# Heads made ready a pair ahead and weight rounding split into two stages in a fused clustered-attention and feed-forward kernel

## The chip, the cores and the metric

The kernel runs on one core of a Trainium2 chip. The metric is device microseconds (us) of one execution, the median of the runs. In this text PE is the matrix engine (TensorE), DVE the vector engine, ACT the scalar engine, POOL the general-purpose engine (GpSimd), and SP the engine that only issues DMAs. Each engine works through its own queue in order and waits for the others by semaphores.

## The reference

Attention in which a query sees only keys of its own cluster, followed by a feed-forward layer whose activation is h - tanh(h):

```python
# q, k, v: (4, 8, 768, 64) f32; centroids: (8, 16, 64) f32
q_assign = argmax(q_n @ c_n.T)          # nearest of 16 centroids of the head, by cosine
k_assign = argmax(k_n @ c_n.T)
mask = q_assign[:, :, :, None] == k_assign[:, :, None, :]
scores = where(mask, (q @ k.T) / 8, -1e9)
attn = softmax(scores)
x = (attn @ v).transpose(0, 2, 1, 3).reshape(3072, 512)
h = x @ w_in                            # w_in (512, 2048), float64 in memory
out = (h - tanh(h)) @ w_out             # w_out (2048, 512), float64 in memory
```

## The kernel before

Two heads make a pair (128 partitions: 2 heads of 64 dimensions); there are 4 batches of 4 pairs, pairs n = 0 to 15. Queries are taken in two halves of 384. The main loop runs over 96 **steps** `(n, half, s)`: for each batch, each half, each of its 4 pairs, and each of 3 thirds of the keys (s = 0, 1, 2; two key tiles of 128 each). Twelve steps, all of one batch and half, are called a **block** here, blocks 0 to 7. Step k runs on the engines in this order:

- `begin(following)`: the scores of step k+1. PE multiplies two key tiles with the queries into PSUM tiles `sc` (pool `ps_s`, two buffers), ACT takes the exponential in place (L317).
- `value`: PE multiplies the weights `e` of step k with the values (L348). After the last third, `total` adds up the denominators on PE (`den`, L361), ACT copies both results, POOL tests each denominator against two bounds (L371 and L372, twice each), and DVE later divides (`divide`, three reciprocals L378 and a product L381).
- `select` of step k+1: DVE multiplies the exponentials with the test "query's cluster code equals key's cluster code" (L326, four instructions, into `e`, two buffers), POOL adds the rows of `e` up (L335, L339).
- Beside these, the feed-forward layer of the block before (`ffn_items`, 28 items spread over the 12 steps: 16 `up` items with `h` on PE L393, tanh on ACT L398 and `g = h - tanh` on DVE L400, then 12 `project` items with `o` on PE L406). Block 0 has no such work; the items of block 7 run after the last step, as a tail.

Work to be done by DVE and so on in step k (`todo`) is handed out between the feed-forward items of that step through `between`: an item's matmuls come first, then its share of `todo`, then the `g` of an `up` item.

**Preparing a pair** (`prepare`, stages 0 to 3): `turn` transposes q and k on PE into two `ps_s` tiles (L233) and copies q with ACT (L239), k with DVE (L241); `similar` multiplies with the centroids (L251) and ACT copies (L256); `route` transposes on PE (L263) and takes the arg-max in four DVE instructions (L271 to L278); `publish` transposes the codes of the queries on PE (L287), DVE copies them, and SP writes them to memory (`q_codes`); `spread` reads them back into all partitions (`row`). Stages 0 to 2 run in the thirds s = 0, 1, 1 and stages 3 and `spread` at the start of s = 2 of the step group just before the pair is first used. So pairs 1, 2, 3 of a batch are prepared in its first half (even block), pair 0 of the next batch at the end of the second half (odd block).

**The weights** lie in memory as float64 and are rounded to f32 by hand in 32 pieces (`round_weights`): ACT scales the low words (L146), DVE builds the bits in two instructions (L147, L151), POOL adds (L154), DVE masks small numbers in two more (L155, L159). One piece per step in block 0, three per step in block 1. Pieces are fetched by POOL's DMA queue into two `raw` buffers. Projections, `h`, have two PSUM banks (`ps_f`).

The first lines issue the loads: q and k of pair 0, v of pair 0, q and k of pair 1, the other v, and last the centroids; then the centroid norms on DVE, then pair 0 is prepared.

## Time and profile before

| | |
|---|---|
| runs | median 1259.69 us, 1257.97 to 1261.23 |
| profiled execution | 1258.72 us, span of its instructions 1256.9 us |
| PE busy | 1084.5 us (86% of the span) |
| DVE busy | 530.5 us (42%) |
| POOL busy | 486.7 us (39%) |
| ACT busy | 294.4 us (23%) |
| chain of work that ended last | PE 76%, DVE 14%, POOL 5%, the rest 1% or less each |

The profile is read by stretches, because the stages have different limits: the start, up to the first `select` (at 39.74 us); block 0, which has no feed-forward work; block 1, in which two thirds of the weights are rounded; blocks 2 to 7; and the tail. For each stretch one asks how busy PE is, and where it is not, what ended its waits. Spans of POOL are rough. The rows for this stand in the section after the next.

### The profile page before, as it was taken

To read this page: it belongs to the slowest core of one execution; us is meant where nothing else is said; L and a number is where in the kernel's file an instruction comes from. 1 tells how busy PE (TensorE), PEld (TensorE's weight loads), DVE (VectorE), ACT (ScalarE), POOL (GpSimd) and SP (SyncE) were. 2 spreads that over 40 slices of the span, in tenths; PEclk is the share of its full clock that TensorE was granted. 3 is DMA by queue.
4 is the path that set the end of the run, shared out by engine and by line. 5 is a ranking of instruction groups with operands and counts; after the bars stand their busy time and mean duration, and the time that the engine had idled before them with its cause. 6 is when DMAs were issued, how large, how long until landed. Compare 5 with 4: busy or idle time off the path is not lost.

```text
span 1256.9 us, 10657 instructions
## 1 busy us (share of the span) xinstructions
PE 1084.5 (86%) x3842; PEld 503.2 (40%) x3842; DVE 530.5 (42%) x902; ACT 294.4 (23%) x475; POOL 486.7 (39%) x358
## 2 busy tenths in 40 slices
PE   1554587688989899999988999999898899999997
PEld 1222133333444434544344434544444344544553
DVE  1666676676334433443335332443343433442210
ACT  1222232222123212222222222322222212321110
POOL 0455475565323343353333433454232343444000
PEclk9777778888999999999999999999999999999999
DMA  6232214231211101111111110012110001000000
GB/s 158 58 86 68 77 65 125 84 109 55 59 34 38 38 34 29 26 26 41 48 38 26 38 42 21 26 26 55 42 31 12 10 33 34 13 9 9 9 8 20
DMA packets 88525, 55.44 MB, mean 44 GB/s; under 512 B 77008, under 2 KB 77200, under 8 KB 88464
## 3 DMA queue, kind: packets, MB, share of 16 engines
q1 hardware_dynamic: 83856, 37.89, 11.4%
q0 software_dynamic: 4608, 16.78, 4.3%
q8 instruction: 33, 0.54, 0.2%
q14 instruction: 28, 0.23, 0.1%
HBM read 48.27 MB, written 6.39 MB: 43 GB/s over the span
## 4 chain that ended last, share of the span: by engine, by line
PE 76%; DVE 14%; POOL 5%; ACT 1%; issue 1%; DMA 1%; SPq 1%; POOLq 0%; DVEq 0%; ACTq 0%
PE o L406 26%; PE h L393 24%; PE sc L312 11%; PE av L348 10%; POOL rest L154 3%; DVE w_in L151 2%; DVE e L326 2%; PE pt L233 2%; PE den L361 2%; SPq L223 1%; DVE den L378 1%; POOL is_in L371 1%; PE sim L251 1%; DVE w_in L147 1%; DVE w_out L151 1%
## 5 line engine op out<-in xcount | busy, mean ns | idle before, releaser
L393 PE MATMUL h<-xT,w_in 128*128 128x384 f32 x1024 | 354.7, 501 | 26.3 <-DVE g L400 26.3
L339 POOL TENSOR_TENSOR sum<-sum,e 128x768 f32<-128x768 f32 x128 | 232.1, 1813 | 348.9 <-DVE e L326 346.4
L406 PE MATMUL o<-w_out,g 128*128 128x512 f32 x768 | 343.7, 599 | 0.0
L326 DVE SCALAR_TENSOR_TENSOR e<-row,code,sc 128x384 f32<-128x384 f32 x384 | 213.2, 608 | 229.6 <-ACT sc L317 99.8
L393 PEld LDWEIGHTS h<-xT,w_in 128*128 128x128 f32 x1024 | 193.6, 194 | 183.3 <-issue 34.6
L406 PEld LDWEIGHTS o<-w_out,g 128*128 128x128 f32 x768 | 141.6, 190 | 187.1 <-issue 186.0
L317 ACT ACTIVATE sc<-sc 128x768 f32<-128x768 f32 x192 | 145.9, 793 | 271.2 <-PE sc L312 270.6
L312 PE MATMUL sc<-t,t 64*128 64x384 f32 x768 | 173.4, 571 | 37.0 <-DVE e L326 23.3
L400 DVE TENSOR_TENSOR g<-h,th 128x384 f32<-128x384 f32 x128 | 71.1, 556 | 224.0 <-ACT th L398 223.8
L371 POOL TENSOR_SCALAR is_in<-den 128x384 f32<-128x384 f32 x64 | 75.0, 1171 | 222.0 <-ACT den L368 219.0
L348 PE MATMUL av<-e,vals 128*64 128x384 f32 x768 | 158.3, 537 | 0.0
L398 ACT ACTIVATE th<-h 128x384 f32<-128x384 f32 x128 | 62.7, 490 | 321.1 <-PE h L393 321.1
L312 PEld LDWEIGHTS sc<-t,t 64*128 64x128 f32 x768 | 73.3, 206 | 123.2 <-issue 74.7
L378 DVE RECIPROCAL den<-den 128x128 f32<-128x128 f32 x96 | 83.3, 917 | 57.1 <-POOL is_in L371 57.1
L348 PEld LDWEIGHTS av<-e,vals 128*64 128x64 f32 x768 | 50.2, 147 | 101.8 <-issue 98.0
L335 POOL TENSOR_TENSOR sum<-e 128x768 f32<-128x768 f32 x32 | 57.8, 1806 | 40.2 <-DVE e L326 40.2
L372 POOL TENSOR_TENSOR ok<-ok,is_in 128x384 f32<-128x384 f32 x64 | 63.8, 997 | 5.3
L413 ACT COPY osb<-o 128x512 f32<-128x512 f32 x24 | 14.0, 585 | 168.8 <-PE o L406 168.8
L233 PE MATMUL pt<-ident,x 128*128 128x128 f32 x192 | 30.0, 304 | 26.1 <-issue 16.3
L287 PE MATMUL sim<-ident,code 128*12 128x128 f32 x16 | 5.1, 320 | 48.7 <-DVE code L278 48.7
L233 PEld LDWEIGHTS pt<-ident,x 128*128 128x128 f32 x192 | 24.9, 156 | 35.6 <-issue 22.4
L241 DVE COPY t<-pt 128x768 f32<-128x768 f32 x16 | 15.3, 956 | 40.8 <-PE pt L233 40.8
(60 smaller groups left out, 368.6 us busy)
## 6 DMA issues: line engine op xcount, KB each, us to landing
row<-q_codes SPq DMA_DIRECT2D x32, 384.0 KB
raw<-in_moe_w_in_dram POOLq DMA_DIRECT2D x16, 512.0 KB, 4.2
raw<-in_moe_w_out_dram POOLq DMA_DIRECT2D x16, 512.0 KB, 3.8
x<-in_q_dram SPq DMA_DIRECT2D x32, 192.0 KB
x<-in_k_dram SPq DMA_DIRECT2D x32, 192.0 KB
vals<-in_v_dram SPq DMA_DIRECT2D x32, 192.0 KB
out_dram<-osb SPq DMA_DIRECT2D x24, 256.0 KB
q_codes<-qc SPq DMA_DIRECT2D x16, 6.0 KB
```

What stands on the lines that cost most here:

```text
L233: nc.tensor.transpose(out=pt[:, j // HCH, (j % HCH) * P : (j % HCH + 1) * P], in_=x[:, j].rearrange("p h d -> p (h d)"), identity=ident,)
L312: nc.tensor.matmul(sc[:, h, 0:TB], lhsT=turned[n, 1][r].rearrange("p a n -> p (a n)")[:, j * P : (j + 1) * P], rhs=turned[n, 0][r, half], ...
L317: nc.scalar.activation(out=sc[:, :, 0:TB], in_=sc[:, :, 0:TB], func=ACT.Exp, scale=SCALE)
L326: nc.vector.scalar_tensor_tensor(out=e[:, h], in0=rows[n, half][:, h], scalar=codes[n][:, 1, j // HCH, h, j % HCH : j % HCH + 1], in1=sc[: ...
L339: nc.gpsimd.tensor_tensor(out=s, in0=s, in1=pair[:, i], op=ALU.add)
L348: nc.tensor.matmul(avs[n, half][h * D : h * D + D], lhsT=vals[n][:, j, h], rhs=e[:, i, h], start=(j == 0), stop=(j == NCH - 1),)
L371: nc.gpsimd.tensor_scalar(out=is_in, in0=t, scalar1=bound, scalar2=None, op0=op)
L372: nc.gpsimd.tensor_tensor(out=ok, in0=ok, in1=is_in, op=ALU.mult)
L378: nc.vector.reciprocal(out=t[:, c], in_=t[:, c])
L393: nc.tensor.matmul(h, lhsT=w_in[i][:, c, o * P : (o + 1) * P], rhs=xT[b, half][:, c], start=(c == 0), stop=(c == CD - 1),)
L400: nc.vector.tensor_tensor(out=gs[i][:, o], in0=h, in1=th, op=ALU.subtract)
L406: nc.tensor.matmul(acc[sub], lhsT=gs[i][:, o, sub * P : (sub + 1) * P], rhs=w_out[i][:, o], start=(i == 0 and o == 0), stop=(i == NQ4 - 1 ...
```

## The change

- **Pairs a pair ahead.** The stages of a pair are put on a list (`ready`) that assigns them to steps: pairs 0 and 1 before the loop, pairs 2 and 3 in block 0, pairs 4, 5, 6 in block 1; from then on pair 3 of a batch in the first three steps of its even block, and pairs 0, 1, 2 of the next batch in the odd block. The stages go to the end of the step's `todo`, `turn` copies both q and k with ACT, and `spread` is issued two steps before use. The codes travel as bf16.
- **Start.** Centroids are loaded first, on ACT's queue; three weight pieces are fetched at once; q and k of pair 1 come before v of pair 0; the transposes of pair 0 stand ahead of the centroid norms; two pieces are rounded before the loop. v is loaded with the heads apart, so that each partition gets 1536 bytes in a row.
- **Weight rounding in two stages.** `round_weights` ends with POOL's addition, and the last two DVE instructions (`guard_weights`) run one call later; three `raw` buffers; `rest` shares the output's buffers.
- **Range check by sums.** In place of four POOL instructions per pair and half, POOL adds the denominators up (`wholes`) and their reciprocals (`inverses`); the bounds are tested once at the end.
- **PSUM.** `ps_f` gets three banks and also holds `den`; `ps_a` keeps one.
- **Output stores** move from SP's queue to POOL's.

The core of the diff:

```diff
-        rawp = cx.enter_context(tc.tile_pool(name="rawp", bufs=2))
+        rawp = cx.enter_context(tc.tile_pool(name="rawp", bufs=3))
-        ps_a = cx.enter_context(tc.tile_pool(name="ps_a", bufs=2, space=PSUM))
-        ps_f = cx.enter_context(tc.tile_pool(name="ps_f", bufs=2, space=PSUM))
+        ps_a = cx.enter_context(tc.tile_pool(name="ps_a", bufs=1, space=PSUM))
+        ps_f = cx.enter_context(tc.tile_pool(name="ps_f", bufs=3, space=PSUM))
...
             nc.gpsimd.tensor_tensor(out=rest, in0=bits, in1=rest, op=ALU.add)
+
+        def guard_weights(n: int):
...
+            hi = raws.pop(n).rearrange("p (n two) -> p n two", two=2)[:, :, 1]
             nc.vector.tensor_scalar(
                 out=bits, in0=hi, scalar1=20, scalar2=0x7FF,
                 op0=ALU.logical_shift_right, op1=ALU.bitwise_and,
             )
             nc.vector.scalar_tensor_tensor(
-                out=dst, in0=bits, scalar=float(F32_LEAST), in1=rest.bitcast(F32),
+                out=dst, in0=bits, scalar=float(F32_LEAST), in1=rests.pop(n).bitcast(F32),
...
-            is_in = okp.tile([P, TB], F32, name="is_in")
-            for bound, op in ((SUM_LEAST, ALU.is_ge), (SUM_MOST, ALU.is_le)):
-                nc.gpsimd.tensor_scalar(out=is_in, in0=t, scalar1=bound, scalar2=None, op0=op)
-                nc.gpsimd.tensor_tensor(out=ok, in0=ok, in1=is_in, op=ALU.mult)
+            nc.gpsimd.tensor_tensor(out=wholes, in0=wholes, in1=t, op=ALU.add)
...
+                nc.gpsimd.tensor_tensor(out=inverses, in0=inverses, in1=dens.pop((n, half)), op=ALU.add)
...
+        def before(n: int):
+
+            yield lambda: (turn(n, 0, nc.scalar), turn(n, 1, nc.scalar), load(n + 2))
+            yield lambda: similar(n)
+            yield lambda: route(n)
+            yield lambda: publish(n)
...
+            if b == 0:
+                at = (p - 2) * NS + 1
+            elif p < HP - 1:
+                at = ((2 * b - 1) * HP + p + 1) * NS
+            else:
+                at = 2 * b * HP * NS
+            for i, stage in enumerate(before(n)):
+                ready.setdefault(at + i - (i > 1), []).append((i, stage))
...
+            if guarded < rounded - 1 or guarded == len(PIECES) - 1:
+                guard_weights(guarded)
+                guarded += 1
+                fetch()
...
+        centroid_load()
+        load(0)
+        for i in range(3):
+            fetch()
+        constants()
+        load(1)
...
+        turn(0, 0, nc.scalar)
+        turn(0, 1, nc.vector)
+        centroid_norms()
+        similar(0)
+        turn(1, 0, nc.scalar)
+        load(2)
+        route(0)
+        publish(0)
+        spread(0, 0)
+        weights_on()
         begin(steps[0])
+        turn(1, 1, nc.scalar)
+        load(3)
+        similar(1)
+        weights_on()
         for i in range(2):
             select(*steps[0][:2], i)
+        route(1)
+        publish(1)
...
+            if 3 in stages:
+                stages.pop(3)()
+            if after and after[2] == 0:
+                spread(*after[:2])
...
+            todo += [stages[i] for i in sorted(stages)]
```

What this makes of the order of instructions, at two places. First DVE in block 1, where three pieces of the weights are rounded in a step (`w_in_70`, `w_out_71` and the like are pieces of the two weight matrices, `raw` the fetched words, `rest` POOL's sum, `g` the activation). Before:

```order
L147 TENSOR_SCALAR w_in_70<-raw 128x512
L151 SCALAR_TENSOR_TENSOR w_in_70<-raw,w_in_70 128x512
L155 TENSOR_SCALAR w_in_70<-raw 128x512
L159 SCALAR_TENSOR_TENSOR w_in_70<-w_in_70,rest 128x512
L400 TENSOR_TENSOR g<-h,th 128x384
L147 TENSOR_SCALAR w_out_71<-raw 128x512
L151 SCALAR_TENSOR_TENSOR w_out_71<-raw,w_out_71 128x512
L155 TENSOR_SCALAR w_out_71<-raw 128x512
L159 SCALAR_TENSOR_TENSOR w_out_71<-w_out_71,rest 128x512
```

Now, where the last piece of `w_in` and the first of `w_out` meet:

```order
L146 TENSOR_SCALAR w_out_72<-raw 128x512
L150 SCALAR_TENSOR_TENSOR w_out_72<-raw,w_out_72 128x512
L162 TENSOR_SCALAR w_in_71<-raw 128x512
L166 SCALAR_TENSOR_TENSOR w_in_71<-w_in_71,rest 128x512
L409 TENSOR_TENSOR g<-h,th 128x384
```

The two last instructions of a piece now stand behind the two first of the next piece.

Second PE in block 2, at the preparation of a pair (`pt` are the transposes of `turn`, `sim<-t` the product of `similar`, `sim<-ident,simt` the transposes of `route`, `sim<-ident,code` that of `publish`, `sc` and `av` scores and values, `h` the feed-forward layer). Before:

```order
L393 MATMUL h<-xT,w_in_67 128x384 x8
L233 MATMUL pt<-ident,x_624 128x128 x6
L233 MATMUL pt<-ident,x_627 128x128 x6
L393 MATMUL h<-xT,w_in_67 128x384 x4
L312 MATMUL sc<-t_1430,t_1439 128x384 x4
...
L251 MATMUL sim<-t_1594,bd 32x384 x2
L251 MATMUL sim<-t_1603,bd 32x384 x2
L393 MATMUL h<-xT,w_in_68 128x384 x4
L263 MATMUL sim<-ident,simt 128x128 x3
L287 MATMUL sim<-ident,code 12x128
L312 MATMUL sc<-t_1594,t_1603 128x384 x4
```

Now:

```order
L402 MATMUL h<-xT,w_in_68 128x384 x12
L244 MATMUL pt<-ident,x_1366 128x128 x6
L244 MATMUL pt<-ident,x_1369 128x128 x6
L323 MATMUL sc<-t_1139,t_1148 128x384 x4
...
L402 MATMUL h<-xT,w_in_69 128x384 x8
L262 MATMUL sim<-t_1672,bd 32x384 x2
L262 MATMUL sim<-t_1681,bd 32x384 x2
L274 MATMUL sim<-ident,simt 128x128 x3
L298 MATMUL sim<-ident,code 12x128
L323 MATMUL sc<-t_1355,t_1364 128x384 x4
```

The feed-forward matmuls that stood between the stages now stand ahead of them; `publish` follows `route` directly, as before, with nothing of another item between.

## Rows read from the trace of the kernel before

**Rows 1.** Busy time by stretch: length, PE, PEld, DVE, ACT, POOL; clock, DMA, GB/s.
```profile
39.74:182.31 142.57, 81.43 (x310) 33.44 (x311) 92.72 (x134) 35.82 (x53) 77.40 (x61) 0.74 0.25 72
182.31:286.22 103.91, 74.58 (x235) 35.06 (x234) 72.66 (x121) 28.21 (x50) 59.82 (x55) 0.89 0.35 106
286.22:349.86 63.64, 59.87 (x209) 25.11 (x209) 29.47 (x47) 14.64 (x23) 29.24 (x20) 0.95 0.19 52
349.86:1167.29 817.43, 776.71 (x2835) 362.65 (x2834) 318.08 (x542) 199.94 (x323) 318.24 (x215) 0.99 0.11 30
1049.11:1167.29 118.18, 118.18 (x409) 55.21 (x410) 44.72 (x76) 27.87 (x46) 51.55 (x35) 1.00 0.04 13
1167.29:1256.90 89.61, 82.59 (x226) 42.30 (x224) 10.00 (x19) 10.19 (x20) 0.00 (x0) 0.98 0.04 13
...
349.86:496.31 146.45, 135.13 (x507) 63.21 (x505) 57.49 (x98) 35.57 (x57) 53.34 (x36) 0.98 0.13 34
```

**Rows 2.** Timeline of the start: start, length, engine, line, operation [idle before, releaser].
```profile
20.88 0.23 DVE L178 TENSOR_TENSOR sq<-cen 128x64 f32<-128x64 f32 x1 [19.33 <-DMA cen<-in_centroids_dram]
...
25.15 2.77 PE L233 MATMUL pt<-ident,x 128*128 128x128 f32 x12
...
39.74 2.19 DVE L326 SCALAR_TENSOR_TENSOR e<-row,code,sc 128x384 f32<-128x384 f32 x4 [4.96 <-DMA row<-q_codes]
```

**Rows 3.** DMA queue of the loads, 2 to 9 us: packets, MB, share.
```profile
q1 hardware_dynamic: 3214, 0.81, 54.3%
```

**Rows 4.** Timeline of DVE and POOL at the end of block 0.
```profile
163.57 2.18 DVE L326 SCALAR_TENSOR_TENSOR e<-row,code,sc 128x384 f32<-128x384 f32 x4
164.86 3.75 POOL L339 TENSOR_TENSOR sum<-sum,e 128x768 f32<-128x768 f32 x2 [1.07 <-DVE e L326]
...
166.98 2.17 DVE L151 SCALAR_TENSOR_TENSOR w_in<-raw,w_in 128x512 uint32<-128x512 uint32 x1
...
169.30 1.26 POOL L154 TENSOR_TENSOR rest<-w_in,rest 128x512 uint32<-128x512 uint32 x1 [0.69 <-DVE w_in L151]
...
170.59 0.43 DVE L155 TENSOR_SCALAR w_in<-raw 128x512 uint32<-128x512 uint32 x1 [1.44 <-POOL rest L154]
171.05 0.69 DVE L159 SCALAR_TENSOR_TENSOR w_in<-w_in,rest 128x512 f32<-128x512 uint32 x1
...
171.66 2.19 DVE L326 SCALAR_TENSOR_TENSOR e<-row,code,sc 128x384 f32<-128x384 f32 x4
...
179.11 0.69 DVE L151 SCALAR_TENSOR_TENSOR w_in<-raw,w_in 128x512 uint32<-128x512 uint32 x1
```

**Rows 5.** Timeline of DVE, one pair of block 0.
```profile
106.15 2.19 DVE L326 SCALAR_TENSOR_TENSOR e<-row,code,sc 128x384 f32<-128x384 f32 x4 [4.59 <-DMA row<-q_codes]
111.11 2.58 DVE L378 RECIPROCAL den<-den 128x128 f32<-128x128 f32 x3 [2.78 <-POOL is_in L371]
...
144.16 2.19 DVE L326 SCALAR_TENSOR_TENSOR e<-row,code,sc 128x384 f32<-128x384 f32 x4 [4.99 <-DMA row<-q_codes]
```

**Rows 6.** Timeline of DVE in block 1, one piece to the next.
```profile
190.89 0.42 DVE L147 TENSOR_SCALAR w_in<-raw 128x512 uint32<-128x512 uint32 x1
...
194.56 0.43 DVE L147 TENSOR_SCALAR w_in<-raw 128x512 uint32<-128x512 uint32 x1
```

**Rows 7.** Timeline of PE at three preparations, in blocks 0, 2 and 3.
```profile
96.15 0.55 PE L263 MATMUL sim<-ident,simt 128*128 128x128 f32 x3 [0.61 <-ACT simt L256]
...
375.54 0.38 PE L287 MATMUL sim<-ident,code 128*12 128x128 f32 x1 [3.08 <-DVE code L278]
375.85 2.93 PE L312 MATMUL sc<-t,t 64*128 64x384 f32 x8
...
611.57 0.28 PE L287 MATMUL sim<-ident,code 128*12 128x128 f32 x1 [2.49 <-DVE code L278]
611.77 1.56 PE L312 MATMUL sc<-t,t 64*128 64x384 f32 x8
613.26 1.51 PE L348 MATMUL av<-e,vals 128*64 128x384 f32 x8
```

More of the change, by code (lines that the diff above doesn't have):

```diff
@@ L41 @@
 EPS = 1e-9
-SUM_LEAST = 2.0**-5
+MOST_INVERSE = 2.0**5
 SUM_MOST = 2.0**80
@@ L87 @@
     bd = const.tile([P, HP, 2 * C], F32, name="bd")
-    ok = const.tile([P, TB], F32, name="ok")
+    inverses = const.tile([P, TB], F32, name="inverses")
+    wholes = const.tile([P, TB], F32, name="wholes")
     flag = const.tile([1, 1], I32, name="flag")
@@ L138, in round_weights @@
                 return
-            dst = PIECES[n][0]
-            w = FQ * P
-            raw = raws.pop(n)
-            pair = raw.rearrange("p (n two) -> p n two", two=2)
+            bits = PIECES[n][0].bitcast(U32)
+            pair = raws[n].rearrange("p (n two) -> p n two", two=2)
             lo, hi = pair[:, :, 0], pair[:, :, 1]
-            rest = rawp.tile([P, w], U32, name="rest")
-            bits = dst.bitcast(U32)
+            rest = rests[n] = outp.tile([P, FQ * P], U32, name="rest", tag="osb")
             nc.scalar.activation(out=rest, in_=lo, func=ACT.Copy, scale=2.0**-29)
@@ L297, in spread @@
         def spread(n: int, half: int):
-            t = rows[n, half] = qbp.tile([P, 2, TB], F32, name="row")
+            t = rows[n, half] = qbp.tile([P, 2, TB], BF16, name="row")
             nc.sync.dma_start(
@@ L358, in total @@
             s = sums.pop((n, half))
-            ps = ps_a.tile([P, TB], F32, name="den", tag="a")
+            ps = ps_f.tile([P, TB], F32, name="den", tag="f")
             for h in range(2):
@@ L477, in fast @@
             following = steps[at + 1] if at + 1 < len(steps) else None
+            after = steps[at + 2] if at + 2 < len(steps) else None
+            block = 2 * b + half
             if p == 0 and s == 0:
-                block = 2 * b + half
                 fill = ffn_items((block - 1) // 2, (block - 1) % 2) if block else []
@@ L482, in fast @@
             now = [fill.pop(0) for _ in range(-(-len(fill) // left))]
-            nxt = n + 1 if half == 0 and p + 1 < HP else (b + 1) * HP if half == 1 and p + 1 == HP else None
-            if nxt is not None and s == NS - 1:
-                prepare(nxt, 3)
+            stages = dict(ready.get(at, []))
+            if 3 in stages:
+                stages.pop(3)()
+            if after and after[2] == 0:
+                spread(*after[:2])
             if following:
@@ L501, in fast @@
                 todo += [weights_on] * (1 if block == 0 else 3)
-            pre = [lambda: None] * 4
-            if nxt is not None:
-                pre = [lambda st=st: prepare(nxt, st) for st in range(4)]
-            if half == 1 or (half == 0 and p == HP - 1):
-                m = b * HP + p + 1 if half == 1 and p + 1 < HP else b * HP if half == 0 else None
-                if m is not None and s == 0:
-                    spread(m, 1)
+            todo += [stages[i] for i in sorted(stages)]
             slots = max(len(now), 1)
@@ L532, in fast @@
             it(lambda: None)
-        least = const.tile([P, 1], F32, name="least")
-        nc.vector.tensor_reduce(out=least, in_=ok, axis=AX.X, op=ALU.min)
+        for t, bound in ((inverses, MOST_INVERSE), (wholes, SUM_MOST)):
+            nc.vector.tensor_scalar(out=t, in0=t, scalar1=bound, scalar2=None, op0=ALU.is_le)
+        nc.vector.tensor_tensor(out=wholes, in0=wholes, in1=inverses, op=ALU.mult)
+        fine = const.tile([P, 1], F32, name="fine")
+        nc.vector.tensor_reduce(out=fine, in_=wholes, axis=AX.X, op=ALU.min)
         pl = ps_a.tile([1, P], F32, name="pl", tag="a")
-        nc.tensor.transpose(out=pl, in_=least, identity=ident)
+        nc.tensor.transpose(out=pl, in_=fine, identity=ident)
         nc.vector.tensor_reduce(out=flag, in_=pl, axis=AX.X, op=ALU.min)
```

114 lines of the change are left out of this document (48 added, 66 removed).

## Prediction

> **What bounds the kernel now.** I read the busy time by stretch first [rows 1], then in each stretch the timeline of the engine that is late. Blocks 2 to 7 (349.86 to 1167.29 us) are bound by PE: busy 776.7 of 817.4 us at a clock of 0.99. Block 7 shows the floor: 118.18 us, PE never idle, no pair prepared in it. It lacks two scores and one value product that the other blocks have, 1.5 us each [rows 7], so a block without preparation is 118.2 + 4.5 = 122.7 us. Five such and block 7 make 731.7 us; the rest of the 817.4, some 86 us, is the price of 11 preparations there, 7.8 us each. The tail is PE's. Block 0 (39.74 to 182.31, counted from the first select to the select of step 13) is not: PE 81 of 143 us at a granted clock of 0.74, a mean of its two levels 1.2 and 2.4 GHz, DVE 93, POOL 77, no engine full. There DVE waits for a transfer or for POOL [rows 5] or is held up beside POOL [rows 4]. In block 1 (to the select of step 19 at 286.22) DVE is busy 72.7 of 103.9 us and waits for POOL once in every piece [rows 4]. So gains can come from the start, from waits of DVE in blocks 0 and 1, and from bubbles of PE at preparations later.
>
> **How DVE and POOL share.** [Rows 4] decide the size of the weight term. L151 has two operands in SBUF; it takes 0.69 us when POOL is idle (at 179.11) and 2.17 us at 166.98, where POOL's two sums run from 164.86 to 168.61: it ends at 169.15, 0.54 us after them. So it stood still until POOL was through. L326, with one operand in PSUM, runs beside the sums at its usual 0.55 us each. In the new order L166, again with two operands in SBUF, comes 0.46 us behind L150, and POOL's addition (1.26 us) starts 0.15 us behind L150 (169.15 to 169.30). No row shows these two together, since L159 always waited for the addition. Bounds: not held, L162 and L166 take 0.43 + 0.69 + gaps = 1.15 us; held like L151, they end 0.15 + 1.26 + 0.55 = 2.0 us behind L150. I take 2.0, from the nearest row. The old path is 1.44 of waiting and 1.15 = 2.6 us. The split then saves 0.55 us a piece, not 1.44: the wait turns into a hold.
>
> The Trainium skill, "SBUF — State Buffer", section "Who interferes with whom", says that a DVE instruction with two SBUF inputs and a GpSimd instruction that reads SBUF exclude each other, the later one standing still until the first is through. The trace agrees for L151 beside POOL's sums (2.17 against 0.69 us); for L166 beside the addition no run here shows it. By this rule the sum below holds; without it the total would be some 25 us lower, which is the first rival.
>
> **Start: first select from 39.74 to 28.0.** The chain began with the centroids, which arrived behind all loads at 20.88 [rows 2]. They now come early, and the chain begins with q and k of pair 0. By 9 us 0.81 MB of 256-byte packets had moved on that queue [rows 3], just these four loads of 192 KB. The third weight piece (0.5 MB) now competes, for 0 to 3.5 us; I take 1.5 and 10.5 us. Then the transposes of k (half of 2.77), its copy (1.0), and from the norms on the old 18.86 us (20.88 to 39.74) less the 2.8 us of transposes that lie ahead now, and less 1.0 for `similar`, which need not wait for the copy, and for rows of half the bytes: 10.5 + 1.4 + 1.0 + 15.1 = 28.0. The two pieces rounded here lie under the transfer of the codes (4.96 us of idle DVE). Range 26 to 32. The four loads of pair 2 now stand on SP's queue ahead of the write of the codes; they go out when pair 0 is turned, some 12 us before that write, and four such loads took 7 us beside the weights [rows 3], so they are through.
>
> **Block 0: 142.6 to 123 us.** After the first select the second pair is finished in line: the transposes of k need the PSUM tile that the select frees, then copy, products, copy, transposes, arg-max 2.3, `publish`, scores, exponential: some 11 us, where the next select once came after 3.9. That is the price of being ahead. Then 12 selects to the one of step 13. A step with one piece and nothing else took 8.1 us (163.57 to 171.66) and takes 8.1 - 0.55 = 7.6; eight are 61. Two steps with a division but no preparation took 10.65 (171.66 to 182.31), and lose the wait for the range check (1.66 there) and 0.55, but the new addition `inverses`, about 1 us, holds the next L150 for 0.6: 9.1 each, 18. Two steps have a division, an arg-max and a `publish`. Here DVE waits about 2.3 us for `den` (the row transfer that used to cover it is gone), divides 3.2, rounds 3.7, takes the arg-max 2.3, and after `publish` waits 2.9 for scores and exponential: with its select 16.5 each, 33. A preparing trio then is 2 x 7.6 + 16.5 = 31.7 against 38.0 before (106.15 to 144.16, rows 5), in which the row transfer's 5 us and 2.78 for the range check fall away. Sum 11 + 61 + 18 + 33 = 123. PE is not late: its work in a trio at the half clock of this stretch is some 24 us. Range -10 to +10.
>
> **Block 1 to the select of step 19: 103.9 to 98.5 us.** 18 pieces before and now. From piece to piece it was 3.67 us [rows 6] and becomes 3.67 - 0.55 = 3.1: -9.5. The waits for the range check go, -1.9. Pair 4 is now prepared here, arg-max and the wait behind `publish`: +4.5. `inverses` twice: +1.3. A third `raw` buffer does not hurry the pieces: its fetch is issued only after POOL's addition, and I count at most 0.3 us of waiting. The 6 steps give 98.3.
>
> **Step 19 to block 2: 63.6 to 70.5 us.** The old stretch held two pieces and one preparation; now it holds pairs 5 and 6. PE waits for the select of step 19 to turn pair 5 (3.3 us from the stretch's start); then five steps of 10.0 (two with `den`, 0.65 more), 51.3; the rest of pair 5 and all of pair 6, 12.6; scores and values 3.0: 70.2.
>
> **Blocks 2 to 7: 817.4 to 797.8 us.** Nine preparations instead of 11. What does one cost? Block 2 [rows 1] has three: 146.45 - 122.7 = 23.8, or 7.9 each, of which 135.13 - 122.7 = 12.4, or 4.1 each, is busy PE and the rest waiting. The waits were 3.1 for the arg-max at `publish` (2.49 where no `g` stands ahead on DVE, rows 7) and 0.9 at the transposes. `publish` still follows `route` directly, so the 2.49 stays; and since `route` follows `similar` directly now, 0.61 for ACT's copy is laid open (as at 96.15). The transposes' wait shrinks to about 0.3, ACT making both copies. 2.49 + 0.61 + 0.3 + 4.0 = 7.4 each, 66.6 in all, against 86. Of the 4.0 some 3.1 is work and the rest clock: behind 3.08 us of waiting eight score matmuls took 2.93 us, behind 2.49 they took 1.56 [rows 7]. How the clock goes behind 0.61, a 0.55 us piece of work and 2.49, no row shows: 6.5 to 9.3 us a preparation, -8 to +17 in all. The PSUM banks, POOL's relief and the smaller rows change nothing where PE is never idle for them.
>
> **Tail: 89.6 us as before.** The last store goes out on POOL, idle there; -1 to +1.
>
> **Sum.** 28.0 + 123 + 98.4 + 70.3 + 797.9 + 89.6 = 1207.2, and 1.8 us around the span (1258.72 - 1256.9) make 1209.0 against 1258.7. The profiled execution lay 1 us under the median of 1259.7, so 1210.
>
> **Rivals.**
> *The split pays in full.* L166 runs beside POOL's addition: 0.85 us less in each of 30 pieces inside the loop, 1185. Against it stands L151 [rows 4], for it only that the rows show sums of 1.8 us, not this addition.
> *Preparations cost more than counted.* The three of a batch now lie in one odd block with all stages at a step's end, behind the last matmuls, so every wait is PE's. If the half clock follows each (9.3 us, +17) and the 16.5 us steps stretch by 2 each (+4), the time is 1231.
> *The stores stop POOL.* POOL's queue now holds 24 stores, each waiting for ACT's copy of an output that PE has only just finished; behind them are queued the sums of the next step and `wholes`, on which `den`, DVE's division and the buffers of `e` depend. If a store delays the next step by over 50/24 = 2.1 us it eats the gain; at 2.5 each the time is 1270, slower than before. Against it: the sums (3.75 us) have a step of 10.0 us, and they stand ahead of the store in the queue.
> *The change does not do what it says.* If DVE, ahead by a pair, waited for scores in the same places, only the start would be left: about 1248 less the two preparations saved, 1232; this falls in the second rival's place.
>
> **How the numbers follow.** Forecast 1210: 0.50. Split in full, 1185: 0.20. Preparations dearer, or gains of block 0 missing, about 1231: 0.22. Stores or another new wait, 1257 and above: 0.08. The forecast's own bounds, added as independent (start 3, block 0 10, clock 12), reach some 16 us either way. The range that holds 8 in 10 goes from 1184 to 1236. About 0.3% (4 us) is what can be told from no change here: faster 0.92, same 0.03, slower 0.05.
>
> **What would show it.** In the profile after: the first select at 28; the select of step 13 near 151; L166 at about 1.5 us, not 0.69, where POOL adds beside it (if 0.69, the first rival); the start of block 2's `h` near 320; block 3 some 22 us longer than block 7 beyond the 4.5, with PE waits of 0.6 and 2.5 us at each preparation; odd blocks about 145, even ones about 130. A wait of POOL's sums behind a store, with PE idle at scores after it, would make the prediction wrong on the slow side; long waits for `raw` would show in ACT's queue.

## The result, and the profile after

The changed kernel took 1225.4 us (median; 1223.8 to 1226.2), against 1259.2 for the one before on the same chip (1259.7 before its fourth run was in): a ratio of 0.973, 95% interval 0.971 to 0.975. The forecast was 1210 with a range of 1184 to 1236, so sign and range held, and the likeliest time was 15 us too low. The profiled execution took 1225.34 us, its span is 1223.6, and the rows below are from it.

Busy time by stretch after the change, with the boundaries that [rows 1] have: first select, select of step 13, select of step 19, block 2's first `h`, start of the tail; the fifth row is block 7 alone. Columns: stretch and length, then PE, PEld, DVE, ACT, POOL busy (instructions), then PE's clock, DMA share, GB/s.

```profile
30.78:150.40 119.62, 74.73 (x304) 31.70 (x305) 104.85 (x132) 37.99 (x56) 71.53 (x55) 0.76 0.28 79
150.40:254.09 103.69, 77.77 (x260) 37.62 (x258) 91.83 (x127) 30.69 (x52) 54.83 (x49) 0.85 0.33 104
254.09:327.11 73.02, 65.17 (x232) 27.52 (x233) 29.06 (x47) 16.73 (x25) 24.45 (x17) 0.93 0.18 49
327.11:1132.13 805.02, 775.12 (x2786) 361.00 (x2785) 301.87 (x520) 203.46 (x328) 280.51 (x184) 0.98 0.08 23
1014.04:1132.13 118.09, 118.09 (x410) 55.12 (x409) 44.84 (x76) 27.90 (x46) 44.83 (x29) 1.00 0.01 5
1132.13:1223.60 91.47, 82.75 (x226) 42.45 (x224) 10.85 (x21) 10.20 (x20) 2.19 (x4) 0.98 0.04 13
```

Against the forecast:

| stretch | before | forecast | after | miss |
|---|---|---|---|---|
| start, to the first select | 39.74 | 28.0 | 30.78 | +2.8 |
| block 0, to the select of step 13 | 142.6 | 123 | 119.62 | -3.4 |
| block 1, to the select of step 19 | 103.9 | 98.4 | 103.69 | +5.3 |
| step 19 to block 2 | 63.6 | 70.3 | 73.02 | +2.7 |
| blocks 2 to 7 | 817.4 | 797.9 | 805.02 | +7.1 |
| tail | 89.6 | 89.6 | 91.47 | +1.9 |

The select of step 13 comes at 150.40, forecast 151; that is in part luck, since the start is 2.8 us too long and block 0 3.4 too short. The miss of the total comes later: block 1 is no shorter, and a preparation in blocks 2 to 7 costs (805.0 - 731.1) / 9 = 8.2 us, not 7.4 (731.1 is what five blocks of 122.6 and block 7 take without any).

**The weights.** Timeline of DVE after the change, columns as in [rows 4]: a piece of the start, while POOL is idle, and one piece of block 1, up to the next piece.

```profile
29.16 0.69 DVE L166 SCALAR_TENSOR_TENSOR w_in<-w_in,rest 128x512 f32<-128x512 uint32 x1
...
158.40 0.41 DVE L146 TENSOR_SCALAR w_in<-raw 128x512 uint32<-128x512 uint32 x1
158.84 0.69 DVE L150 SCALAR_TENSOR_TENSOR w_in<-raw,w_in 128x512 uint32<-128x512 uint32 x1
159.45 0.42 DVE L162 TENSOR_SCALAR w_in<-raw 128x512 uint32<-128x512 uint32 x1
159.91 1.64 DVE L166 SCALAR_TENSOR_TENSOR w_in<-w_in,rest 128x512 f32<-128x512 uint32 x1
161.47 0.41 DVE L146 TENSOR_SCALAR w_out<-raw 128x512 uint32<-128x512 uint32 x1
```

And POOL's addition beside it:

```profile
159.69 1.30 POOL L153 TENSOR_TENSOR rest<-w_in,rest 128x512 uint32<-128x512 uint32 x1 [1.72 <-DVE w_in L150]
```

L166 is 0.69 us long when POOL is idle and 1.64 beside POOL's addition, which ends at 160.99, 0.56 us before L166 does. The wait of [rows 4] (1.44 us at L155) has gone and a hold of 0.95 us has come: from piece to piece 3.07 us, where it was 3.67 [rows 6].

**A preparation.** Timeline of PE in block 3, from the products with the centroids to the next scores; the brackets are PE's idle time and what ended it.

```profile
508.88 0.85 PE L262 MATMUL sim<-t,bd 128*32 128x384 f32 x8
510.33 0.55 PE L274 MATMUL sim<-ident,simt 128*128 128x128 f32 x3 [0.60 <-ACT simt L267]
513.37 0.38 PE L298 MATMUL sim<-ident,code 128*12 128x128 f32 x1 [2.49 <-DVE code L289]
513.68 2.87 PE L323 MATMUL sc<-t,t 64*128 64x384 f32 x8
```

The two waits are 0.60 and 2.49 us, as forecast. The scores behind them took 2.87 us, at a granted clock of 0.53, where the same eight matmuls take 1.56 at the full clock [rows 7]: the clock is at the lower of its two levels (1.2 and 2.4 GHz) for most of them. Behind all nine preparations of blocks 2 to 7 the scores took 2.34 to 2.93 us.

**Block 1.** Waits of DVE between the selects of steps 13 and 19: waiter, who was waited for, total us, times, longest.

```profile
DVE w_out L146 <- DMA raw<-in_moe_w_out_dram: 3.6, 3, 2.4
DVE e L337 <- ACT sc L328: 2.7, 2, 2.2
DVE den L386 <- POOL wholes L380: 2.3, 1, 2.3
DVE w_out L162 <- POOL rest L153: 1.2, 1, 1.2
```

DVE now stands 3.6 us for raw weights, three buffers or not; before, with two buffers and slower pieces, it was 0.4 in this stretch:

```profile
DVE w_out L147 <- DMA raw<-in_moe_w_out_dram: 0.4, 1, 0.4
```

Timelines of ACT and of PE at the worst place after the change:

```profile
211.42 0.67 ACT L145 ACTIVATE rest<-raw 128x512 uint32<-128x512 uint32 x1 [4.87 <-DMA raw<-in_moe_w_out_dram]
212.00 1.49 ACT L250 COPY t<-pt 128x768 f32<-128x768 f32 x2
```

```profile
202.41 1.47 PE L244 MATMUL pt<-ident,x 128*128 128x128 f32 x12
212.84 2.93 PE L323 MATMUL sc<-t,t 64*128 64x384 f32 x8 [8.95 <-ACT t L250]
```

PE had turned pair 4 at 203.9, but ACT's copies of it (both are ACT's now) stood in its queue behind `rest`, and that behind a transfer: PE idle for 8.95 us.

### The profile page after: what moved, and what is told of

Read it like the earlier page. It is cut to its first block, busy times and chain, and to the rows that moved or that the text cites. A ratio compares the mean times of both kernels' runs of the same rounds, so it can differ in the third digit from the quotient of the medians.

```text
span 1223.6 us, 10558 instructions
## 1 busy us (share of the span) xinstructions
PE 1085.9 (89%) x3842; PEld 506.0 (41%) x3842; DVE 550.4 (45%) x891; ACT 307.3 (25%) x491; POOL 437.3 (36%) x318
## 4 chain that ended last, share of the span: by engine, by line
PE 74%; DVE 12%; issue 9%; ACT 2%; DMA 2%; POOL 1%; SPq 0%; POOLq 0%; DVEq 0%; ACTq 0%
PE o L415 24%; PE h L402 22%; PE sc L323 13%; PE av L359 11%; DVE e L337 2%; PE den L372 2%; PE pt L244 1%; DVE w_in L150 1%; PE sim L262 1%; DVE w_in L166 1%; DVE w_out L150 1%; DMA raw<-in_moe_w_out_dram 1%; DVE den L386 1%; DVE w_in L146 1%; DVE top L287 1%
## 5 line engine op out<-in xcount | busy, mean ns | idle before, releaser
L402 PE MATMUL h<-xT,w_in 128*128 128x384 f32 x1024 | 348.4, 497 | 8.5 <-DVE g L409 8.5
L337 DVE SCALAR_TENSOR_TENSOR e<-row,code,sc 128x384 f32<-128x384 bf16 x384 | 213.3, 608 | 258.5 <-ACT sc L328 198.8
L323 PE MATMUL sc<-t,t 64*128 64x384 f32 x768 | 180.6, 595 | 26.0 <-DVE e L337 14.4
L380 POOL TENSOR_TENSOR wholes<-wholes,den 128x384 f32<-128x384 f32 x32 | 31.8, 993 | 198.0 <-ACT den L379 198.0
L386 DVE RECIPROCAL den<-den 128x128 f32<-128x128 f32 x96 | 83.2, 916 | 35.7 <-POOL wholes L380 35.7
L423 POOL DMA_DIRECT2D out_dram<-osb x24 | 13.4, 558 | 165.0 <-ACT osb L422 165.0
L390 POOL TENSOR_TENSOR inverses<-inverses,den 128x384 f32<-128x384 f32 x32 | 43.8, 1370 | 46.4 <-DVE den L386 46.4
L282 DVE TENSOR_REDUCE mx<-sim 128x24 f32<-128x384 f32 x16 | 8.9, 555 | 73.9 <-PE sim L274 73.9
```

The lines of the kernel that those rows point to most:

```text
L323: nc.tensor.matmul(sc[:, h, 0:TB], lhsT=turned[n, 1][r].rearrange("p a n -> p (a n)")[:, j * P : (j + 1) * P], rhs=turned[n, 0][r, half], ...
L337: nc.vector.scalar_tensor_tensor(out=e[:, h], in0=rows[n, half][:, h], scalar=codes[n][:, 1, j // HCH, h, j % HCH : j % HCH + 1], in1=sc[: ...
L386: nc.vector.reciprocal(out=t[:, c], in_=t[:, c])
L390: nc.gpsimd.tensor_tensor(out=inverses, in0=inverses, in1=dens.pop((n, half)), op=ALU.add)
L402: nc.tensor.matmul(h, lhsT=w_in[i][:, c, o * P : (o + 1) * P], rhs=xT[b, half][:, c], start=(c == 0), stop=(c == CD - 1),)
```

## The experiments

All but the last two undo or change one part of the changed kernel; `own_bank` changes a PSUM bank and an order together. Each was run beside the kernel before (medians of 1258.2 to 1259.4); a ratio is to that kernel, with its 95% interval, and "+" or "-" is the median against 1225.4.

| run | median, us | ratio | against 1225.4 |
|---|---|---|---|
| own_bank | 1175.1 | 0.933 (0.931 to 0.935) | -50.3 |
| filled_waits | 1233.2 | 0.981 (0.979 to 0.983) | +7.8 |
| guard_first | 1214.9 | 0.965 (0.964 to 0.967) | -10.5 |
| one_stage | 1238.5 | 0.984 (0.982 to 0.986) | +13.1 |
| four_raw | 1220.0 | 0.970 (0.968 to 0.972) | -5.4 |
| range_tiles | 1230.0 | 0.977 (0.976 to 0.979) | +4.6 |
| centroids_late | 1231.0 | 0.978 (0.977 to 0.980) | +5.6 |
| in_time | 1228.7 | 0.977 (0.975 to 0.978) | +3.3 |
| banks_back | 1222.5 | 0.970 (0.968 to 0.973) | -2.9 |
| sp_stores | 1225.2 | 0.974 (0.972 to 0.976) | -0.2 |
| combined | 1156.3 | 0.919 (0.917 to 0.921) | -69.1 |
| combined_raw | 1153.4 | 0.916 (0.913 to 0.918) | -72.0 |

### What a preparation costs: own_bank and filled_waits

```diff
-            ps = sims[n] = ps_s.tile([P, 2, 512], F32, name="sim", tag="s")
+            ps = sims[n] = ps_m.tile([P, 512], F32, name="sim", tag="m")
...
-                ready.setdefault(at + i - (i > 1), []).append((i, stage))
+                when = at + i - (i > 1) if b == 0 else at + (-1, 0, 0, 1)[i]
+                ready.setdefault(when, []).append((i, stage))
...
-            todo += [stages[i] for i in sorted(stages)]
+            place = {0: slots - 1, 1: 0, 2: slots - 1, 3: 0}
...
+                mine += [stages[z] for z in sorted(stages) if place[z] == i]
```

(`ps_f` has two banks here, `den` shares `ps_m`.)

> The products with the centroids get a PSUM bank of their own (shared with `den`), and the stages of a preparation of batches 1 to 3 are laid apart so that matmuls of the projections stand between them on PE. Theory: of the 8.15 us that a preparation costs in blocks 2 to 7 only some 3.2 are work; 0.60 and 2.49 are waits and the rest is the half clock that follows them. All but the work goes: nine times 4.5 us in blocks 2 to 7 and twice in the stretch before, 50 us, 1175 us in all, granted clock 0.99 in the odd blocks too. Rival one: the half clock comes with the short matmuls of the preparation itself, not with the waits: only 3.1 us each go, 1191. Rival two: the third bank for the projections was needed, PE then waits for `h` or `o`: 1200 or more.

Measured 1175.1. Timeline of PE at the corresponding preparation of `own_bank`:

```profile
488.00 0.85 PE L263 MATMUL sim<-t,bd 128*32 128x384 f32 x8
488.78 5.43 PE L403 MATMUL h<-xT,w_in 128*128 128x384 f32 x16
494.04 0.49 PE L275 MATMUL sim<-ident,simt 128*128 128x128 f32 x3
494.46 1.56 PE L324 MATMUL sc<-t,t 64*128 64x384 f32 x8
...
497.39 2.85 PE L403 MATMUL h<-xT,w_in 128*128 128x384 f32 x8
500.08 0.27 PE L299 MATMUL sim<-ident,code 128*12 128x128 f32 x1
```

No bracket is left: while ACT copies and DVE takes the arg-max, PE does projections, scores and values, and the scores take 1.56 us. Blocks 2 to 7 last 757.3 us instead of 805.0, so a preparation costs 2.9 us, and its short matmuls alone don't lower the clock: rival one falls. Of the 47.7 us gained there 19.7 are busy time of PE (775.12 to 755.41, with the granted clock at 1.00 and not 0.98) and 28.0 are idle time. Which part the bank has in it and which the order was not run apart. The theory hit the total, not its places: blocks 2 to 7 gave more than the 41 expected, the stretches before them 0.8 instead of 9. In block 1 copies of ACT behind a `rest` still stop PE, 18.8 us in two waits, and in this execution the step of pair 1 in the start was 2.5 us longer, for a reason shown under `sp_stores`.

`filled_waits` asks what of the price was clock. The first call stands in `route` ahead of the transposes, the second in `publish` ahead of its transpose, the last line is what `filler` repeats:

```diff
+            filler(n, ps[:, 1, 0:TB], 1)
...
+            filler(n, ps[:, 0, 0:TB], 4)
...
+                nc.tensor.matmul(out, lhsT=ident, rhs=turned[n, 0][:, 0], start=True, stop=True)
```

> As the changed kernel, but for batches 1 to 3 PE does one matmul of no use (0.67 us) where it waited 0.60 us for the copy and four (2.7 us) where it waited 2.49 us for the arg-max; their results are overwritten. The work that counts is the same. Theory (the half clock follows idle PE): the eight score matmuls behind a preparation take 1.56 us, not 2.93, and the time falls by some 1.7 us a preparation, 11 times, to about 1207. Rival (the half clock comes with the preparation's own short matmuls, or not with the waits at all): no gain, 1225 to 1229.

Measured 1233.2: slower, which neither side had expected. Timeline of PE in block 3 of `filled_waits`, L272 being the filler:

```profile
511.44 0.85 PE L262 MATMUL sim<-t,bd 128*32 128x384 f32 x8
512.89 0.91 PE L272 MATMUL sim<-t,ident 128*128 128x384 f32 x2 [0.60 <-ACT simt L267]
513.64 0.49 PE L279 MATMUL sim<-ident,simt 128*128 128x128 f32 x3
515.44 2.85 PE L272 MATMUL sim<-t,ident 128*128 128x384 f32 x8 [1.31 <-DVE top L289]
518.12 0.27 PE L304 MATMUL sim<-ident,code 128*12 128x128 f32 x1
...
518.33 1.56 PE L329 MATMUL sc<-t,t 64*128 64x384 f32 x8
```

The filler didn't fill: it writes the PSUM tile that ACT and DVE read, so it waited itself (0.60 and 1.31 us) and lengthened the path from products to scores from 4.80 us (508.88 to 513.68) to 6.89. But the clock came back: scores 1.56, and by stretch, block 3 of `filled_waits` and of the changed kernel:

```profile
460.29:608.58 148.29, 141.86 (x537) 67.76 (x535) 55.62 (x97) 37.11 (x60) 47.11 (x31) 1.00 0.14 36
```

```profile
457.73:605.41 147.68, 137.72 (x506) 64.30 (x504) 55.90 (x97) 37.41 (x60) 47.13 (x31) 0.95 0.14 37
```

A granted clock of 1.00 instead of 0.95, with the short matmuls of the preparation unchanged. So the half clock goes with PE's waits: the path is 2.09 us longer, while block 3, with three preparations, is only 0.61 us longer, 0.2 each; some 1.9 us a preparation was clock there. Over blocks 2 to 7 (809.9 us, a price of 8.75) it is 2.09 - 0.55 = 1.5. With 3.3 us of waits (0.60, 2.49, and 0.23 for ACT's copy behind the transposes) and 3.2 of work these make 8.0 to 8.4, about the 8.2. (By the busy time of `own_bank` the clock is 19.7 / 9 = 2.2.)

### The hold: guard_first and one_stage

```diff
+            early = first and guarded < rounded
+            if early:
+                guard_weights(guarded)
+                guarded += 1
+                fetch()
...
                 round_weights(rounded)
...
```

(`first` is set in block 0 alone.)

> In the steps of block 0 the guard of the piece before stands ahead of the rounding of the new one; block 1 unchanged. Theory (a DVE instruction with two SBUF operands stands still while POOL adds): L166 then takes 0.69 us where POOL is idle, or shares the one hold by the sums that L150 has had until now, and POOL's addition runs beside work that it doesn't hold: 0.95 us less in each of 11 steps, 1215. Rival one: L166 is 1.63 us long for a reason of its own (its operands, the buffers): no change, 1225. Rival two: the steps are shorter for DVE but scores or raw data are late next: 1221.

Measured 1214.9; the total is the theory's. Timeline of DVE in `guard_first`, one step of block 0 from the guard to the next select; POOL's two sums run from 78.79 to 82.54, its addition of this piece from 84.31:

```profile
79.43 1.45 DVE L162 TENSOR_SCALAR w_in<-raw 128x512 uint32<-128x512 uint32 x1
80.91 2.18 DVE L166 SCALAR_TENSOR_TENSOR w_in<-w_in,rest 128x512 f32<-128x512 uint32 x1
83.02 0.41 DVE L146 TENSOR_SCALAR w_in<-raw 128x512 uint32<-128x512 uint32 x1
83.46 0.69 DVE L150 SCALAR_TENSOR_TENSOR w_in<-raw,w_in 128x512 uint32<-128x512 uint32 x1
84.07 2.18 DVE L337 SCALAR_TENSOR_TENSOR e<-row,code,sc 128x384 f32<-128x384 bf16 x4
```

What is left is the hold by the sums (it lay on L146 and L150 before), and POOL's addition runs beside L337, which has an operand in PSUM and isn't held. Eight plain steps take 6.58 to 6.75 us instead of 7.52, two with a division 0.5 us less, the other three together 0.4 more; the select of step 13 comes at 142.61 instead of 150.40. So L166 is long because of POOL, not for a reason of its own. The places are not quite the theory's: block 0 gave 7.4 us, not 10.5, and block 1, which was to stay as it was, 2.4; there the waits of DVE for raw data fall from 3.6 to 2.2 us and those for `rest` from 1.2 to nothing.

```diff
-            if guarded < rounded - 1 or guarded == len(PIECES) - 1:
+            if guarded < rounded - (not at_once) or guarded == len(PIECES) - 1:
...
```

(`at_once` is set in the loop; what is left out guards a piece that the start has left over.)

> Rounding as one stage again inside the loop: the guard of a piece stands right behind its rounding; all else as changed (in the start the two first pieces stay as they are). Theory: a piece takes 3.67 us, not 3.07, the wait for POOL's addition comes back in place of the hold of 0.95 us: 30 pieces, +18 us, 1243. Rival: in blocks 0 and 1 the raw data, the scores or ACT are late next, so the split saved little: under +6, 1231.

Measured 1238.5, +13.1: neither +18 nor under +6. In its block 0 a step takes 8.12 us, 0.6 more, as a piece should; timeline of DVE, the guard right behind the rounding:

```profile
57.84 0.43 DVE L162 TENSOR_SCALAR w_in<-raw 128x512 uint32<-128x512 uint32 x1 [1.45 <-POOL rest L153]
58.30 0.69 DVE L166 SCALAR_TENSOR_TENSOR w_in<-w_in,rest 128x512 f32<-128x512 uint32 x1
```

In block 1 its DVE has no wait for raw data at all: the slower pieces are always there in time. So the split's gain of 0.6 us a piece was partly given back as the 3.6 + 1.2 us of waits seen above: block 0 is 7.0 us longer without the split, as 12 pieces should be (7.2), block 1 5.2, where 18 pieces are 10.8 and less the waits 6.0.

### Block 1: four_raw

```diff
-        rawp = cx.enter_context(tc.tile_pool(name="rawp", bufs=3))
+        rawp = cx.enter_context(tc.tile_pool(name="rawp", bufs=4))
...
+        fetch()
         route(0)
...
```

> Four buffers for raw weight pieces instead of three (the fourth piece is fetched ahead of the first arg-max; the squares of the centroids lie in a tile that is in use anyway, to make room). Theory: in block 1 the changed kernel is late by 3.6 us of waits of DVE for raw data, and by ACT standing 12.4 us for it with the copy of pair 4's k queued behind; with a fourth buffer both go, and block 1 up to the select of step 19 takes 99 us, not 103.7: 1221. Rival: `rest`, which has two buffers, or POOL's queue, in which the fetch stands, holds the pieces up as much: 1225.

Measured 1220.0, -5.4; its runs (1218.8 to 1222.3) lie clear of the changed kernel's (1223.8 to 1226.2). By stretch, the selects of step 13 to step 19 in `four_raw`, then its waits of DVE there:

```profile
150.02:247.93 97.91, 75.37 (x260) 36.32 (x258) 92.13 (x127) 30.62 (x52) 54.77 (x48) 0.88 0.35 104
```

```profile
DVE e L337 <- ACT sc L328: 2.2, 1, 2.2
DVE den L386 <- POOL wholes L380: 1.8, 1, 1.8
```

The waits for raw data are gone, and the stretch is 97.9 us (103.69), close to the 98.4 that the prediction had for it. PE still waits once 7.8 us for ACT's copy of pair 4.

### The other parts, undone one by one

```diff
-            nc.gpsimd.tensor_tensor(out=wholes, in0=wholes, in1=t, op=ALU.add)
+            for bound, op in ((SUM_LEAST, ALU.is_ge), (SUM_MOST, ALU.is_le)):
+                nc.gpsimd.tensor_scalar(out=is_in, in0=t, scalar1=bound, scalar2=None, op0=op)
+                nc.gpsimd.tensor_tensor(out=ok, in0=ok, in1=is_in, op=ALU.mult)
```

> The range check per tile again (two comparisons and two products on POOL for every `den`, 4.3 us, instead of two sums), all else as changed. Theory: DVE's division waits 2 to 3 us for POOL at each of the four pair ends of block 0 and about 1 in block 1, less what the addition to `inverses` cost (0.8 us each): +5 to +6, 1231; blocks 2 to 7 unchanged, PE never idle for it. Rival one: POOL's longer work delays the sums and so PE in the later blocks as well: +12 or more. Rival two: DVE is late for other reasons at those places: no change.

Measured 1230.0, +4.6. In its block 0 DVE's division waits 8.2 us for POOL (four times), against 1.2 in the changed kernel; blocks 2 to 7 are no longer (802.7 us), so the first rival falls. (Its step of pair 1 was 2.6 us longer too, see `sp_stores`; without that its block 0 is 4.1 us longer.)

```diff
-        centroid_load()
         load(0)
...
             load(n, (2,))
+        centroid_load()
```

> The centroids are loaded on SP's queue behind the first q, k and v loads, as before the change; all else as changed. Theory: they land near 21 us, the products with them come some 7 us later, the first select near 37.7 instead of 30.78; in block 0 DVE has no slack, so all of it stays: 1232. Rival: what the start loses is made up in blocks 0 and 1 (transfers and POOL further ahead): under +3, 1228.

Measured 1231.0, +5.6. The first select comes at 35.26 us, not 37.7, since the centroids land at 19.2 and not 21; the select of step 13 is 5.5 us late and so is the end (5.6 by the medians): nothing is made up on the way.

```diff
-                at = (p - 2) * NS + 1
+                at = (p - 1) * NS
...
                 stages.pop(3)()
+                if block == 0:
+                    spread(n + 1, 0)
```

> Pairs 2 and 3 of the first batch are prepared only during the pair before them, and their row transfer is issued right behind their codes, as before the change; pair 1 and all else as changed. Theory: DVE stands 3 to 5 us for the row at two places of block 0, where nothing else is late: +8, 1233. Rival: DVE would stand there anyway (for `den`, scores): under +2, 1227.

Measured 1228.7, +3.3, between the two. Timeline of DVE in `in_time`, the first select of pair 2:

```profile
88.21 2.19 DVE L337 SCALAR_TENSOR_TENSOR e<-row,code,sc 128x384 f32<-128x384 bf16 x4 [4.34 <-DMA row<-q_codes]
```

The wait for the row is back. In block 0 waits for rows sum to 9.5 us against 0.9, but the wait for scores that hid behind it falls from 6.6 to 2.2: 8.6 - 4.4 = 4.2, about the 3.9 us by which the select of step 13 is late. A pair ahead trades a wait of 4.3 to 4.7 us for one of 2.2.

```diff
-        ps_a = cx.enter_context(tc.tile_pool(name="ps_a", bufs=1, space=PSUM))
-        ps_f = cx.enter_context(tc.tile_pool(name="ps_f", bufs=3, space=PSUM))
+        ps_a = cx.enter_context(tc.tile_pool(name="ps_a", bufs=2, space=PSUM))
+        ps_f = cx.enter_context(tc.tile_pool(name="ps_f", bufs=2, space=PSUM))
...
-            ps = ps_f.tile([P, TB], F32, name="den", tag="f")
+            ps = ps_a.tile([P, TB], F32, name="den", tag="a")
```

> PSUM as before the change: two banks for `av` and `den`, two for the projections; all else as changed. Theory (the prediction costed the third bank at nothing, PE being never idle for it where it is the bound): 1225, within 3. Rival: PE now and then waits for `h` behind DVE's `g` in blocks 2 to 7, 0.3 us a step over 70 steps: 1240 or more.

Measured 1222.5 (1219.2 to 1225.9), and its interval overlaps the changed kernel's; blocks 2 to 7 last 804.8 us (805.0), so the rival falls: the third bank brings nothing that can be told.

```diff
-                    nc.gpsimd.dma_start(out_r[b, half * HCH + sub], osb)
+                    nc.sync.dma_start(out_r[b, half * HCH + sub], osb)
```

> Output stores on SP's queue again. Theory: POOL is never late because of the stores; only the last one, which took 1.7 us longer from ACT's copy to the end of the span, matters: 1223.6. Rival: the stores hold up POOL's sums and `wholes`, and so `den` and PE, in blocks 2 to 7: 8 us or more to gain, 1217 or less.

Measured 1225.2: no difference that can be told. Timelines of the last copy and store, first the changed kernel (span 1223.6), then `sp_stores` (span 1223.1):

```profile
1214.85 0.59 ACT L422 COPY osb<-o 128x512 f32<-128x512 f32 x1 [13.19 <-PE o L415]
...
1215.73 0.54 POOL L423 DMA_DIRECT2D out_dram<-osb  x1 [13.23 <-ACT osb L422]
```

```profile
1216.04 0.58 ACT L422 COPY osb<-o 128x512 f32<-128x512 f32 x1 [13.19 <-PE o L415]
...
1216.65 0.33 SPq L423 DMA_DIRECT2D out_dram<-osb  x1
```

From the start of the copy to the end of the span it is 8.75 us with POOL's queue and 7.06 with SP's; the whole tail is 89.8 us instead of 91.5, and it is 89.8 in `combined` and `combined_raw` too, which store by SP. This execution reached the tail 1.2 us later; the medians show no gain. The rival with stores that stop POOL falls: blocks 2 to 7 last 805.0 and 805.2 us.

Why it came later has nothing to do with stores. One instruction of pair 1's arg-max, which took 0.56 us in the changed kernel (at 37.99), was held here beside POOL's first sum:

```profile
38.51 2.40 DVE L287 TENSOR_TENSOR top<-top,down 128x384 f32<-128x384 f32 x1
```

The same happens in `own_bank`, `range_tiles` and `banks_back` (2.42 to 2.54 us), and there the second select comes 13.8 us after the first, in the changed kernel 11.3. Where it happens block 0 is some 2 us longer (121.5 to 121.8 us in the three runs that leave block 0's work as it is), so differences of this size between single traces of the start mean nothing.

### Putting it together: combined and combined_raw

`combined` has the edits of `own_bank`, `guard_first` and `sp_stores`, and besides:

```diff
+            if block == 0 and 3 in stages:
+                todo.append(stages.pop(3))
...
-            yield lambda: (turn(n, 0, nc.scalar), turn(n, 1, nc.scalar), load(n + 2))
+            yield lambda: (turn(n, 0, nc.scalar), turn(n, 1, nc.vector if n >= HP else nc.scalar), load(n + 2))
...
         route(0)
+        turn(1, 1, nc.scalar)
+        load(3)
...
         begin(steps[0])
-        turn(1, 1, nc.scalar)
-        load(3)
         similar(1)
...
-        publish(1)
+        ready[0] = [(3, lambda: publish(1))]
```

> The own bank and the laid-apart stages, the guard first in block 0 and the stores on SP together; besides, the copy of k is DVE's from batch 1 on, in block 0 the codes of pairs 1 to 3 are published behind the selects of the next step, and the products of pair 1 stand ahead of the first select. If the single gains add up (50, 10.5, at most 1.7) and DVE no longer waits 2.2 us for scores at two steps nor finishes pair 1 in line (next select some 6 us after the first, not 11.3), with 0.23 us at nine preparations: 1225 - 50 - 10.5 - 1.7 - 4.4 - 5 - 2 = 1151. Rival: block 0 and block 1 become bound by PE at its half clock or by the raw data, and the gains before 150 us are given back there: 1165.

Measured 1156.3, 8.1% under the kernel before and between the two. The select of step 13 comes at 128.78 us (150.40 in the changed kernel), the second select 5.0 us after the first (11.3); blocks 2 to 7 last 758.7. Block 1 is not better (104.4 us): PE waits 19.3 us in two waits for ACT's copies of a pair, the longer one 10.1.

> The combined version with the fourth raw buffer as well. Theory: block 1 of the combined version still waits for raw data (4.1 us on DVE, and PE 10.1 us once for the copy of pair 4 that stands behind a rounding in ACT's queue); the fourth buffer gives what it gave alone, 5 us: 1151. Rival: in the combined version pair 4's copy waits for ACT behind a rounding in any case and sets block 1's length: 1156.

Measured 1153.4, 2.9 less, between the two: the waits of DVE for raw data are gone and block 1 takes 100.2 us, but PE still waits 15.4 us in two waits for ACT's copies, and DVE once 6.3 us for a tanh of ACT. The interval of its ratio (0.913 to 0.918) just overlaps that of `combined` (0.917 to 0.921).

## Why the prediction was right, and where it was off

**Start** (28.0 forecast, 30.78): right in its mechanism; small counts were off. k of pair 0 was there at 11.6, not 10.5. Six transposes of pair 1 (1.54 us at the half clock, 20.35 to 21.9) stand on PE between the products of pair 0 and their transposes, which come at 21.68 and not at some 21.0, where ACT's copy was done; the step on the norms did not count them. From the norms to that copy 3.2 us fell away, not 3.8, and the rows of half the bytes took no less time (3.7 us from issue to select, 3.6 before).

**Block 0** (123, 119.62): the single steps hold. Pair 1 in line 11.3 (forecast 11), a plain step 7.52 (7.6), a division without a preparation 9.04 (9.1). Steps with division, arg-max and `publish` took 14.7 and 15.3, not 16.5: of the 2.3 us of waiting for `den` only 0.3 and 0.95 came. `centroids_late` and `in_time` agree that what DVE loses here reaches the end.

**L166** was the claim on which most hung, and it held: 1.64 us beside the addition, so the first rival (1185) falls. The prediction's own times, 2.6 less 2.0, make 0.6 us a piece, as measured, though it took 0.55. `guard_first` shows the cause by taking the overlap away. The Trainium skill, "SBUF — State Buffer", section "Who interferes with whom", says that a DVE instruction with two SBUF inputs and a GpSimd instruction that reads SBUF exclude each other; these runs agree (0.69 against 1.64 us for L166).

**Block 1** (98.4, 103.69): the step that failed is the sentence on the third `raw` buffer, "at most 0.3 us of waiting". The pieces did become 3.07 us long, but so the data came too late: 3.6 us of waits for raw data, 1.2 for `rest`, and ACT's queue blocked behind the transfers. `four_raw` gives 97.9, so the rest of that sum came out, though 18 pieces at 0.55 are 9.9 us and not the 9.5 that stand in it. With faster pieces the fetch was late: `one_stage`, with the same three buffers and slower pieces, has no such wait.

**Step 19 to block 2** (70.3, 73.02) and **blocks 2 to 7** (797.9, 805.02): the waits were forecast exactly (0.60 and 2.49), and no `g` stands ahead on DVE. What was mis-sized is the clock, of which the prediction took 0.9 us a preparation (4.0 less 3.1 of work) and offered 9.3 as the bound. It is 1.7 by the price of 8.2 (less 3.3 of waits and 3.2 of work), 1.5 to 1.9 by `filled_waits` and 2.2 by `own_bank`. So the second rival's mechanism was at work, at less than half its size (7.1 of its 17 us). Two preparations at 0.8 more are 1.6 of the 2.7 us by which the stretch from step 19 was missed; the rest was not traced. In the sum itself, 731.7 and nine times 7.4 are 798.3, not 797.9.

The reading of [rows 7], a slow group of scores behind 3.08 us and a fast one behind 2.49, rested on too few rows. The same trace has these, at the end of block 5:

```profile
887.23 0.38 PE L287 MATMUL sim<-ident,code 128*12 128x128 f32 x1 [2.49 <-DVE code L278]
887.54 2.93 PE L312 MATMUL sc<-t,t 64*128 64x384 f32 x8
```

Over the 11 preparations of its blocks 2 to 7 the scores took 1.56 to 2.93 us behind 2.49 (five, mean 2.2) and 1.56 to 2.93 behind 3.08 (six, mean 2.2): the length of that one wait does not tell. After the change, with a wait of 0.60 us shortly before it, all nine took 2.34 or more.

**Tail** (89.6, 91.47): forecast -1 to +1 for the last store on POOL's queue; it is +1.7, by the trace of `sp_stores`.

**Stores that stop POOL**: POOL stood at stores for 165 us in all, and by `sp_stores`, where blocks 2 to 7 are as long, nothing behind them was needed in that time.

**Parts that cost or brought nothing**: the third PSUM bank, as said. Undone singly, two-stage rounding, the range check, the early centroids and pairs 2 and 3 a pair ahead are worth 13.1, 4.6, 5.6 and 3.3 us, 26.6 of the 33.8 us, if such parts may be added up, which was not tested. The rest was not run by itself; the traces show blocks 2 to 7 shorter by 12.4 us with two preparations fewer, and block 1 with what follows longer by 9.2 with two more.

What stays open: why block 1 of `combined_raw` is still late. Its waits name ACT's copies behind a `rest`; a version in which that copy doesn't stand behind a rounding was not tried.

## What to carry to other kernels

When a wait of PE for DVE or ACT recurs, don't shorten it but put other matmuls into it, in a PSUM bank that the wait doesn't need: here a bank and a reordering were worth 50 us, more than the whole change, because the half clock behind the wait goes with it (19.7 of the 47.7 us in blocks 2 to 7). When a two-stage pipeline lets a stage start without waiting, look at what runs at that moment on the engine that can hold it up, here POOL: the order of two DVE groups was worth 10 us. And a stage that is made faster moves the bound to its supply: count the buffers again at the new rate.

## What the runs showed of the hardware

- Some DVE instructions with a single SBUF operand are held too: L162 in `guard_first`, 0.41 us alone, took 1.45 beside the first of POOL's two sums and ended 0.3 us after it; the next one, L166, then stood through the whole second sum. Between these two sums DVE got exactly one of its own. The reciprocals L386, also of one SBUF operand, were not held: 0.94 us beside POOL, 0.90 alone (medians in the changed kernel).
- POOL seems to be held up in turn: the addition to `inverses` takes 1.37 us, the one to `wholes`, of the same shape, 0.99. Beside it stands each time the product L389, two operands in SBUF, which DVE starts just before it; all 32 additions take 1.36 to 1.38 us, those of the late blocks too, where no weights are rounded. No run has the addition without the product, so the cause is argued and not shown. Timelines of DVE and POOL in block 3:

```profile
559.88 0.56 DVE L389 TENSOR_TENSOR xT<-xT,den 128x384 f32<-128x384 f32 x1
559.93 1.37 POOL L390 TENSOR_TENSOR inverses<-inverses,den 128x384 f32<-128x384 f32 x1 [0.92 <-DVE den L386]
```

- After idle times of 0.60 and 2.49 us with 0.55 us of work between them the next eight score matmuls ran at the lower clock; with idle times of 0.60 and 1.31 us and filler matmuls behind each they did not.
